# Splitting the last chunk of the output weights one unit later, and the low parts of two q-weight chunks on GpSimd

## The chip, the cores and the metric

The kernel runs on one core of a Trainium2 chip. The core has five engines that run side by side, each through its own list of instructions in order: TensorE (PE in the profile, its weight loads PEld), VectorE (DVE), ScalarE (ACT), GpSimd (POOL) and SyncE (SP), which here only issues DMA transfers. The metric is the device time of one execution in microseconds, lower is better. The time before is the median of three runs; one further execution was taken by the profiler, and all rows below come from it.

## The reference

Two linear attentions, A and B, with the same input `x` (2048 tokens, 448 features, 16 heads of 28) and their own weights; a gate per token mixes them:

```python
def attention(x, wqkv, w_phi, wo):
    q, k, v = heads(x @ wqkv)                      # 16 heads of 28
    pq, pk = q @ w_phi, k @ w_phi                  # per head, 28 x 28
    phi_q = concat(softmax(pq), softmax(-pq))      # 56 features
    phi_k = concat(softmax(pk), softmax(-pk))
    kv, z = phi_k^T @ v, sum_over_tokens(phi_k)
    o = (phi_q @ kv) / (phi_q @ z + 1e-6)
    return merge(o) @ wo
g = sigmoid((A_x * gate_w).sum(-1))
out = g * attention(A_x, A...) + (1 - g) * attention(A_x, B...)
```

Both attentions read `A_x`. (The excerpt is shortened; `heads` and `merge` stand for reshapes and transposes.)

## The kernel before

**Precision by two parts.** Large products keep float32 accuracy by splitting an operand into a high part, which ScalarE makes by a copy to a rounded type (`high_w`, L133; `high_folded`, L202), and a low part, the difference, which VectorE or GpSimd makes (`low_w`, L136; `low_folded`, L208). A projection of two token tiles (`proj`, L225) is 22 matmuls over such parts.

**Folded weights.** The feature map `w_phi` is multiplied into the q and k weights on the chip. For A this is `fold` (L153, L158, L159). For B the strips of the weights are loaded, multiplied on TensorE (`fold_strips`, L181), transposed by VectorE (`turn_strips`, L189), stored to DRAM (`td`, L191) and loaded again in chunks (`load_folded`, L198), and the chunks are split by `high_folded` and `low_folded`. For the q weights of B there are four chunks, and only two buffers, `bd` and `wps`: chunks 2 and 3 are loaded into the same buffers once the low parts of chunks 0 and 1 have been made.

**Units.** The 16 token tiles are handled in 8 units of two tiles. Every engine gets its instructions in the order in which the program below issues them; a manual schedule keeps that order.

- *Stage 1* (first loop, L476) takes the k and v side of A: per unit the k projection, `k_shift` (L239 to L242: maximum and differences on VectorE, the mirrored half on GpSimd), `k_exp` (L246, ScalarE), `k_sums` (L255, L256 on VectorE, L264 twice on GpSimd: phi of k), the v projection and `v_out` (L272, ScalarE), and a unit late `kv_acc` (L289, TensorE: phi_k against v). Between these lies work that prepares later stages: the split of the output weights, the folded k weights of B, and the first q units of A.
- *Stage 2* (second loop, L584) takes k and v of B and, beside it, q of A: `q_front` (L316, L318 on VectorE, stores L325 to DRAM from the sync and ScalarE queues), `q_load` (L333, the exchanged layout back), `q_exp0` (L341, ScalarE), `q_min` (L345 on VectorE, L349 on GpSimd), `q_exp1` (L356), `q_turn` (L359, VectorE, into `wtb[k % 2]`), `num` (L371, TensorE), then for the unit before `a_turn` (L576, VectorE), `n_rec` (L383 VectorE, L388 and L389 GpSimd), `n_den` (L396), `weights` (L403, L404 GpSimd), `n_mul` (L409) and `a_add` (L413, GpSimd). `weights` needs the gates, which unit 0 computes (L566 to L568) and passes through DRAM (L570, L572).
- *Stage 3* is a written-out list of steps (`STEPS`): q of B, and the output products (L839) against the split output weights.

**The split of the output weights.** The weights are held as seven chunks in DRAM (`wos`). `load_wo(c)` (L459) loads a chunk into a half of `wtb[c // 2 % 2]`; `high_wo(c)` makes the high part on ScalarE (L133), `low_wo(c)` the low part on GpSimd (L136) and then issues two stores to DRAM from the sync queue (L468, L469):

```python
WOS = {3: (0, 1), 5: (4, 5, 2, 3), 6: (6,)}    # L473: unit of stage 1 -> chunks
...
for c in WOS.get(u, ()):                       # L524, after k_exp(u)
    high_wo(c)
    low_wo(c)
```

The load of chunk 6 is issued at the end of unit 5 (L536), when the stores of chunks 2 and 3, whose buffer it takes, have landed; behind it on the sync queue stand the strips of the q weights of B (L539), then, in unit 6, the q stores and the q load of A's second q unit (`FRONTS`, L474). ScalarE and GpSimd meet chunk 6 in unit 6 ahead of `q_exp0(0)`, `q_min(0)` and `q_exp1(0)` (L549 to L552), and GpSimd ahead of `k_sums(6)`, which the program issues in unit 7 ahead of `k_shift(7)`.

**The low parts of chunks 2 and 3 of B's q weights.** Their high parts are made in unit 1 of stage 2 (L595), their low parts on VectorE in unit 2 (L634), after the turn of q and before the `a_turn` of unit 3. They are first needed by the projection that unit 6 of stage 2 issues.

Buffers in PSUM are three pairs of banks that rotate (`two_tile`), so a projection also waits until the engines have read the one before the last but one.

Of the kernel before, what the change touches and what calls it, by code (L numbers as in the profile page):

```python
# [49 lines left out]
def hedgehog_mix(ctx: ExitStack, tc: tile.TileContext, xd, wv, wkt, wqt, wphi, wo, cmask, cpmask, out):  # L50


    nc = tc.nc
# [44 lines left out]
    wq = [wp_.tile([P, 2, 4, D], F32R, name="wqa"), None]  # L98
# [42 lines left out]
    def low_wv(b, c, eng):  # L141
        low_w(wvr[c], wvs[b][:, 0, c], wvs[b][:, 1, c], eng)
# [3 lines left out]
    def two_tile(i=None):  # L146
        if i is None:
            i = turn[0] = (turn[0] + 1) % 3
        return twos[i].tile([P, 2, 512], F32, name=f"two{i}")
# [35 lines left out]
    def turn_strips(wt, ts, i):  # L185
        t = wt[:, :4 * D]
        o = t.rearrange("p (j i w m) -> p i w j m", i=2, w=2, m=HP)
        for j, ps in enumerate(ts):
            nc.vector.transpose(o[:, j], ps[:, :, :D].rearrange("p w (j m) -> p w j m", m=HP))  # L189
        for g in range(4):  # L190
            nc.sync.dma_start(td[i][:, g * P:g * P + P].rearrange("(j t) x -> t j x", t=HP),  # L191
                              t[HP * g:HP * g + HP].rearrange("t (j x) -> t j x", x=P))
# [7 lines left out]
    def high_folded(bufs, dst, cs):  # L200
        for c in cs:
            nc.scalar.activation(dst[:, 0, c].rearrange("p (h f) -> p h f", f=DH),  # L202
                                 bufs[c].rearrange("p (h m) -> p h m", m=HP)[:, :, :DH], AF.Copy)

    def low_folded(bufs, dst, cs, eng):
        for c in cs:
            h, l = [dst[:, i, c].rearrange("p (h f) -> p h f", f=DH) for i in range(2)]
            eng.tensor_tensor(l, bufs[c].rearrange("p (h m) -> p h m", m=HP)[:, :, :DH], h.bitcast(F32), OP.subtract)  # L208
# [7 lines left out]
    def proj(u, w, ps, order=None):  # L216
        n = w.shape[3]
        for i, j in order or [(i, j) for i in range(2) for j in range(11)]:
            if i is None:
                warm(j)  # L220
                continue
            t = 2 * u + i
            x, o = xg[t // 4], (t % 4) * P
            xc, k, wc = TERMS[j]
            nc.tensor.matmul(ps[:, i, :n], x[:, xc, o:o + P], w[:, k, wc], start=j == 0, stop=j == 10)  # L225
        return ps
# [17 lines left out]
    def k_exp(k):  # L244
        for s in range(2):
            nc.scalar.activation(es[k][:, s], es[k][:, s], AF.Exp)  # L246
# [19 lines left out]
    def k_sums(k):  # L266
        k_sums0(k)
        k_sums1(k)
# [12 lines left out]
    def kv_acc(k):  # L281
        b, u = divmod(k, NU)
        v, phi = vs[k % 2], phis.pop(k)
        for w in range(2):
            for g in range(4):
                for r in range(4):
                    h = 4 * r + g
                    hs = (w * H + h) * DH
                    nc.tensor.matmul(kvp[b][32 * r:32 * r + DH + 1, g], v[:, w, h // 2, h % 2], phi[:, :, hs:hs + DH],  # L289
                                     start=(u == 0 and w == 0 and g == 0), stop=(u == NU - 1 and w == 1),  # L290
                                     skip_group_check=True)

    def state_copy(b):
        nc.scalar.activation(kvs[b][:, :, :, :DH], kvp[b].rearrange("p g s f -> p s g f"), AF.Copy)
# [9 lines left out]
    def state_turn(b):  # L304
        state_turn0(b)
        state_turn1(b)
# [20 lines left out]
    def q_front(k, ps):  # L327
        q_diff(k, ps)
        q_store(k, nc.sync)
        q_store(k, nc.scalar)  # L330

    def q_load(k):
        nc.sync.dma_start(tq[k % 2].rearrange("p c g w f -> p (c g w f)"), qd[k].rearrange("r t c x -> (r t) (c x)"))  # L333
# [6 lines left out]
    def q_exp0(k):  # L340
        nc.scalar.activation(eq[:, 0, :, :, :DH], tview(k), AF.Exp)  # L341

    def q_least(k):
        mn = work.tile([P, 4, 8], F32, name="qmn")
        nc.vector.tensor_reduce(mn, tq[k % 2].rearrange("p c g w f -> p c (g w) f"), AX.X, OP.min)  # L345
        return mn

    def q_rest(k, mn):
        nc.gpsimd.tensor_tensor(eq[:, 1, :, :, :DH], mn.rearrange("p c a -> p a c")[:, :, :, None].to_broadcast([P, 8, 4, DH]),  # L349
                                tview(k), OP.subtract)  # L350

    def q_min(k):
        q_rest(k, q_least(k))

    def q_exp1(k):
        nc.scalar.activation(eq[:, 1, :, :, :DH], eq[:, 1, :, :, :DH], AF.Exp)  # L356

    def q_turn(k):
        nc.vector.transpose(wtb[k % 2], eq.rearrange("p s a c f -> p (s a c f)"))  # L359
        eTs[k] = wtb[k % 2].rearrange("p (s g t) -> p s g t", s=2, g=4)  # L360
# [30 lines left out]
    def n_rec(k):  # L391
        n_rec0(k)
        n_rec1(k)

    def n_den(k):
        nc.vector.reciprocal(sms[k][2], sms[k][2])  # L396

    def weights(k, eng):
        b, u = divmod(k, NU)
        rs, dd, den = sms[k]  # L400
        gt = gate[:, b, :, 2 * u:2 * u + 2].rearrange("p c n -> p n c")
        d4 = den.rearrange("p r (n c) -> p r n c", n=2)
        eng.tensor_tensor(d4, d4, gt[:, None].to_broadcast([P, 4, 2, 4]), OP.mult)  # L403
        eng.tensor_tensor(dd, rs, den[:, :, None, :].to_broadcast([P, 4, 2, 8]), OP.mult)  # L404

    def n_mul(k, lo=0, hi=8):
        c3 = cview(k).rearrange("p r s a m -> p (r s) a m")[:, :, lo:hi, :DH]
        dd = sms[k][1].rearrange("p r s a -> p (r s) a")[:, :, lo:hi, None]
        nc.gpsimd.tensor_tensor(c3, c3, dd.to_broadcast([P, 8, hi - lo, DH]), OP.mult)  # L409
# [51 lines left out]
    def high_wo(c):  # L461
        st = wo_part(c)
        high_w(st[0], st[1].bitcast(F32R))
# [6 lines left out]


    WVS = {2: (0, 1), 3: (2, 3)}
    WOS = {3: (0, 1), 5: (4, 5, 2, 3), 6: (6,)}  # L473
    FRONTS = {2: 0, 5: 1}  # L474
    pq = None
    for u in range(NU):  # L476
# [45 lines left out]
        for c in WVS.get(u, ()):  # L522
            low_wv(1, c, nc.gpsimd)
        for c in WOS.get(u, ()):  # L524
            high_wo(c)
# [48 lines left out]
    def a_turn(k):  # L574
        for i, t in enumerate(nums[k]):
            nc.vector.transpose(ctr[k % 2][:, 1024 * i:1024 * i + 1024], t.rearrange("p i t -> p (i t)"))  # L576
        nums.pop(k)
# [6 lines left out]
    for u in range(NU):  # L584
        k = NU + u
        f, m, n = u + 2, u + 1, u - 1
        if u == 2:
            ctr[1] = mid.tile([P, 2048], F32, name="ctr")
        pq = proj(f % NU, wq[f // NU], two_tile())
        if n >= 0:  # L590
            a_turn(n)
            n_rec(n)
        q_exp0(m)
        if u == 1:
            high_folded(fq, wq[1], (2, 3))  # L595
        q_min(m)
        if u == 0:
            turn_strips(wtqb, pf, 1)
        q_exp1(m)
        if n >= 0:  # L600
            n_den(n)
            weights(n, nc.gpsimd)
            if u > 1:
                n_mul(n)
        else:
            k_sums(k - 1)
        q_front(f, pq)
        q_load(f)
        pk = proj(u, wk[1], two_tile())
        if u == 0:  # L610
            kv_acc(k - 1)
            state_copy(0)
        else:
            k_sums(k - 1)
            if u == 1:
                n_mul(n)
        k_shift(k, pk)
        if u == 0:
            state_turn(0)
            q_turn(m)  # L620
        pv = proj(u, wvs[1], two_tile())
        v_out(k, pv)
        k_exp(k)
        if u == 0:
            fq = [wp_.tile([P, 512], F32, name=n) for n in ("bd", "wps")] * 2
            for cs in ((0, 1), (2, 3)):
                load_folded(1, fq, cs)
                if cs[0] == 0:
                    high_folded(fq, wq[1], cs)
                    low_folded(fq, wq[1], cs, nc.gpsimd)  # L630
        else:
            q_turn(m)
        if u == 2:
            low_folded(fq, wq[1], (2, 3), nc.vector)  # L634
        if u == NU - 1:
            woh, wol = [wp_.tile([P, 7, D], F32R, name=n) for n in ("wkb", "wvb")]
            for w, d in ((woh, wod[0]), (wol, wod[1])):
                nc.sync.dma_start(w.bitcast(F32), d)
        if n >= 0:
            a_add(n)  # L640
        if u == 4:
            nc.gpsimd.tensor_scalar(gate[:, 1], gate[:, 0], -1.0, 1.0, op0=OP.mult, op1=OP.add)
        ts = nums[u] = [two_tile(), two_tile()]
        num(u, [t[:, i] for t in ts for i in range(2)])
        if u == 0:
            gates()
        else:
            kv_acc(k - 1)
# [261 lines left out]
```

## Time and profile before

| | us |
|---|---|
| median of 3 runs (lowest, highest) | 355.02 (354.36, 358.86) |
| profiled execution | 357.44 |
| its span | 355.7 |
| TensorE busy in the span | 345.7 |
| VectorE busy | 276.2 |
| GpSimd busy | 264.6 |
| ScalarE busy | 122.0 |

The profile names a group of instructions by line, engine, operation, and the program's names of what is written and read. In a timeline a row has the start in us from the span's start, the time from the first start to the last end, engine, line, operation, shape and count; in brackets stands the idle time of the engine before it and what ended that. "SPq" is the sync queue's issue of a DMA; the transfer itself runs on. The chain of waits is followed back from the last instruction, at each step to what released it or to the instruction before it on its engine. Rows of stretches give the busy time of each engine, with the number of instructions in parentheses, the granted clock of TensorE as a share of full speed, the busy share of the DMA engines and the bytes that they moved per second.

### The profile page before, as it was taken

How to read it: one execution, taken by the hardware profiler on the slowest of the kernel's cores; microseconds unless marked ns; L12 is line 12 of the kernel's file. 1: busy time of each engine (PE TensorE's matmuls, PEld its weight loads, DVE VectorE, ACT ScalarE, POOL GpSimd, SP SyncE). 2: the span in 40 equal slices, each digit the busy share in tenths (PEclk: the TensorE clock that was granted, in tenths of full speed). 3: DMA queues.
4: the chain of work that ended last, by engine and by line, in shares of the span. 5: the costliest groups of instructions: out<-in, count | busy, mean ns of one | idle time of the engine just before them, and what ended most of it. 6: DMA issues, size and time to landing. Idle time of an engine off the chain costs nothing.

```text
span 355.7 us, 8516 instructions
## 1 busy us (share of the span) xinstructions
PE 345.7 (97%) x3599; PEld 301.6 (85%) x3599; DVE 276.2 (78%) x319; ACT 122.0 (34%) x176; POOL 264.6 (74%) x230
## 2 busy tenths in 40 slices
PE   8999999999969999999999999999999999999995
PEld 7999888889867888888798989888888978888894
DVE  4328765666776769799999898899899999988840
ACT  4525445126334052222244131412224454334331
POOL 2453799795574346995989788896779999999850
PEclk9999999999996999999999999999999999999999
DMA  8795236865744633141322333158672562664111
GB/s 242 224 332 143 103 99 201 216 163 185 187 101 110 162 102 100 55 131 53 103 77 82 105 105 98 61 188 330 170 233 68 153 177 77 178 173 129 53 53 52
DMA packets 39022, 49.58 MB, mean 139 GB/s; under 512 B 11848, under 2 KB 32168, under 8 KB 38696
## 3 DMA queue, kind: packets, MB, share of 16 engines
q1 hardware_dynamic: 33832, 44.90, 42.7%
q10 hardware_dynamic: 5152, 4.13, 3.7%
q8 instruction: 28, 0.46, 0.5%
q14 instruction: 10, 0.08, 0.1%
HBM read 29.27 MB, written 21.36 MB: 142 GB/s over the span
## 4 chain that ended last, share of the span: by engine, by line
PE 73%; DVE 11%; POOL 8%; DMA 3%; issue 3%; ACT 1%; POOLq 0%; DVEq 0%; ACTq 0%
PE two L225 44%; PE out L839 16%; PE two L371 4%; PE kv L289 3%; POOL e L264 3%; DMA wtb<-wos 2%; PE two L153 2%; PE two L434 2%; POOL wva L409 2%; DVE wva L576 1%; DVE wtb L359 1%; DVE sm L255 1%; DMA wod<-wtb 1%; PE two L181 1%; DVE wka L208 1%
## 5 line engine op out<-in xcount | busy, mean ns | idle before, releaser
L225 PE MATMUL two<-wka,xg 128*128 128x448 f32 x352 | 73.8, 365 | 0.0
L225 PEld LDWEIGHTS two<-wka,xg 128*128 128x128 f32 x352 | 65.1, 188 | 6.4 <-issue 0.8
L264 POOL TENSOR_TENSOR e<-e,rs 128x896 f32<-128x896 f32 x32 | 53.8, 1705 | 16.3 <-DVE rs L256 16.3
L272 ACT ACTIVATE vs<-two 128x896 f32<-128x896 f32 x16 | 14.7, 918 | 82.3 <-PE two L225 77.8
L255 DVE TENSOR_REDUCE sm<-e 128x32 f32<-128x896 f32 x32 | 33.0, 1071 | 8.7 <-ACT e L246 8.7
L225 PE MATMUL two<-wva,xg 128*128 128x450 f32 x176 | 39.3, 373 | 0.1
L225 PE MATMUL two<-wqa,xg 128*128 128x448 f32 x176 | 39.2, 379 | 0.0
L225 PEld LDWEIGHTS two<-wqa,xg 128*128 128x128 f32 x176 | 33.6, 194 | 5.0 <-ACT e L246 1.5
L359 DVE STREAM_TRANSPOSE wtb<-xrb 128x2048 f32<-128x2048 f32 x16 | 36.6, 2289 | 1.5 <-ACT xrb L356 1.5
L246 ACT ACTIVATE e<-e 128x896 f32<-128x896 f32 x32 | 28.7, 945 | 26.5 <-POOL e L242 26.4
L225 PE MATMUL two<-wvb,xg 128*128 128x448 f32 x176 | 37.2, 366 | 0.0
L242 POOL TENSOR_TENSOR e<-mx,e 128x896 f32<-128x896 f32 x16 | 27.3, 1706 | 13.0 <-DVE mx L241 12.8
L225 PE MATMUL two<-wkb,xg 128*128 128x448 f32 x176 | 36.7, 363 | 0.1
L225 PEld LDWEIGHTS two<-wva,xg 128*128 128x128 f32 x176 | 33.1, 190 | 3.2 <-issue 0.3
L225 PEld LDWEIGHTS two<-wvb,xg 128*128 128x128 f32 x176 | 33.0, 188 | 2.8
L225 PEld LDWEIGHTS two<-wkb,xg 128*128 128x128 f32 x176 | 32.9, 188 | 2.8 <-DVE wva L576 0.5
L839 PE MATMUL out<-wkb,e 128*128 128x448 f32 x154 | 34.7, 369 | 0.1
L839 PEld LDWEIGHTS out<-wkb,e 128*128 128x128 f32 x154 | 28.5, 188 | 4.1 <-issue 0.8
L349 POOL TENSOR_TENSOR xrb<-qmn,tq 128x896 f32<-128x896 f32 x16 | 28.2, 1762 | 3.5 <-issue 1.9
L409 POOL TENSOR_TENSOR wva<-wva,cdd 128x896 f32<-128x896 f32 (+1 forms) x12 | 26.5, 2212 | 0.8
L409 POOL TENSOR_TENSOR ctr<-ctr,cdd 128x896 f32<-128x896 f32 (+1 forms) x12 | 26.5, 2212 | 0.6
L239 DVE TENSOR_REDUCE mx<-two 128x32 f32<-128x896 f32 x16 | 16.8, 1048 | 11.8 <-PE two L225 11.8
(117 smaller groups left out, 586.3 us busy)
## 6 DMA issues: line engine op xcount, KB each, us to landing
tq<-qd SPq DMA_DIRECT2D x16, 448.0 KB
qd<-uq ACTq DMA_DIRECT2D x32, 112.0 KB
qd<-uq SPq DMA_DIRECT2D x32, 112.0 KB
od<-wva SPq DMA_DIRECT2D x8, 448.0 KB
wqa<-od SPq DMA_DIRECT2D x8, 448.0 KB
wod<-wtb SPq DMA_DIRECT2D x14, 224.0 KB
xrb<-in_xt SPq DMA_DIRECT2D x2, 1024.0 KB
out<-bd SPq DMA_DIRECT2D x8, 224.0 KB
```

The costliest lines, as they stand in the source:

```text
L225: nc.tensor.matmul(ps[:, i, :n], x[:, xc, o:o + P], w[:, k, wc], start=j == 0, stop=j == 10)
L239: nc.vector.tensor_reduce(mx[:, 0], p4, AX.X, OP.max)
L242: nc.gpsimd.tensor_tensor(e5[:, 1], mx[:, 1, :, :, None].to_broadcast([P, 2, H, DH]), e5[:, 0], OP.subtract)
L246: nc.scalar.activation(es[k][:, s], es[k][:, s], AF.Exp)
L255: nc.vector.tensor_reduce(sm[:, s], e[:, s].rearrange("p (h f) -> p h f", f=DH), AX.X, OP.add)
L264: nc.gpsimd.tensor_tensor(e3, e3, rs[:, s, :, None].to_broadcast([P, HA, DH]), OP.mult)
L272: nc.scalar.activation(v[:, :, :, :, :DH].rearrange("p w j q f -> p w (j q) f"), hb(ps[:, :, :D]), AF.Copy)
L349: nc.gpsimd.tensor_tensor(eq[:, 1, :, :, :DH], mn.rearrange("p c a -> p a c")[:, :, :, None].to_broadcast([P, 8, 4, DH]), tview(k), OP.sub ...
L359: nc.vector.transpose(wtb[k % 2], eq.rearrange("p s a c f -> p (s a c f)"))
L371: nc.tensor.matmul(banks[r][32 * g:32 * g + 32, 256 * s:256 * s + 256], kvt[b][32 * r:32 * r + 32, s, g], eT[32 * r:32 * r + 32, s, g], st ...
L409: nc.gpsimd.tensor_tensor(c3, c3, dd.to_broadcast([P, 8, hi - lo, DH]), OP.mult)
L839: nc.tensor.matmul(outs[t % 2][:, :D], (hi, lo)[x][:, c], w[:, c], start=x == 0 and n == 0 and c == 0, stop=x == 1 and c == 6)
```

## The change

Chunk 6 of the output weights is split in unit 7 of stage 1 instead of unit 6: its high part on ScalarE, its low part on GpSimd and its two stores on the sync queue move, the load does not. The low parts of chunks 2 and 3 of the folded q weights of B are made on GpSimd in unit 1 of stage 2, behind that unit's `q_min`, instead of on VectorE in unit 2. Nothing is added or taken away.

```diff
-    WOS = {3: (0, 1), 5: (4, 5, 2, 3), 6: (6,)}
+    WOS = {3: (0, 1), 5: (4, 5, 2, 3), 7: (6,)}
...
         if u == 1:
             high_folded(fq, wq[1], (2, 3))
         q_min(m)
+        if u == 1:
+            low_folded(fq, wq[1], (2, 3), nc.gpsimd)
...
         else:
             q_turn(m)
-        if u == 2:
-            low_folded(fq, wq[1], (2, 3), nc.vector)
         if u == NU - 1:
```

## The prediction

> **What bounds the kernel now.** I read the page's table of engines first, then the chain of waits, then the order of time on each engine around the two edits. Stage 1 is the first loop over units, stage 2 the second, stage 3 the written-out list.
>
> ```profile
> PE 345.7 (97%) x3599; PEld 301.6 (85%) x3599; DVE 276.2 (78%) x319; ACT 122.0 (34%) x176; POOL 264.6 (74%) x230
> ```
>
> TensorE is busy nearly throughout, so an edit on other engines pays only where TensorE waits or runs slowly. The chain of waits (start us, us, what) leaves TensorE at two places that the change touches:
>
> ```profile
> 91.55 8.00 DMA wtb<-wos
> ...
> 100.31 1.16 POOL wtb L136
> ...
> 103.13 3.37 POOL e L264 x2
> ...
> 160.87 3.09 DVE wka L208 x2
> 163.96 2.30 DVE wva L576 x2
> ```
>
> The first place is unit 6 of stage 1: the load of chunk 6 of the output weights takes 8.00 us, GpSimd's split of it (L136) waits for that, and the normalising of the k features of that unit (L264) waits behind on the same engine. The second is unit 2 of stage 2, where the low parts (L208) take 3.09 us of VectorE. TensorE in order of time, from three stretches:
>
> ```profile
> 58.44 1.51 PE L181 MATMUL two<-wtb,wps 28*32 28x448 f32 x32
> ...
> 80.10 4.76 PE L225 MATMUL two<-wqa,xg 128*128 128x448 f32 x22
> 84.70 4.57 PE L225 MATMUL two<-wka,xg 128*128 128x448 f32 x22
> ...
> 99.15 4.66 PE L225 MATMUL two<-wva,xg 128*128 128x450 f32 x22
> 106.55 1.72 PE L289 MATMUL kv<-e,vs 128*29 128x56 f32 x64 [2.74 <-POOL e L264]
> 108.20 1.81 PE L181 MATMUL two<-ctr,wps 28*32 28x448 f32 x32
> 109.94 6.02 PE L225 MATMUL two<-wqa,xg 128*128 128x448 f32 x22
> 115.79 4.57 PE L225 MATMUL two<-wkb,xg 128*128 128x448 f32 x22
> 120.29 0.99 PE L289 MATMUL kv<-e,vs 128*29 128x56 f32 x64
> ...
> 127.42 4.75 PE L225 MATMUL two<-wqa,xg 128*128 128x448 f32 x22
> ...
> 160.33 4.75 PE L225 MATMUL two<-wqa,xg 128*128 128x448 f32 x22
> ...
> 177.90 4.75 PE L225 MATMUL two<-wqa,xg 128*128 128x448 f32 x22
> ...
> 193.82 4.75 PE L225 MATMUL two<-wqa,xg 128*128 128x448 f32 x22
> ```
>
> At 103.81 TensorE stops for 2.74 us, and what follows is slow: the k-v products take 1.72 instead of 0.99, the strips 1.81 instead of 1.51, the projection 6.02 instead of 4.76, together 2.29 more. Waiting and slowness make 5.03 us. The stretches of 1 us (PE, PEld, DVE, ACT, POOL busy, granted clock, DMA share, GB/s) name the slowness:
>
> ```profile
> 105.00:106.00 1.00, 0.00 (x0) 0.00 (x0) 1.00 (x1) 0.03 (x1) 1.00 (x1) 0.96 1.00 215
> 106.00:107.00 1.00, 0.45 (x20) 0.45 (x24) 0.51 (x1) 0.00 (x0) 1.00 (x2) 0.50 0.83 253
> 107.00:108.00 1.00, 1.00 (x56) 1.00 (x48) 0.19 (x1) 0.00 (x0) 1.00 (x1) 0.50 1.01 385
> ...
> 112.00:113.00 1.00, 1.00 (x5) 0.90 (x4) 1.00 (x2) 0.00 (x0) 0.00 (x0) 0.62 0.00 0
> ```
>
> The granted clock falls to half shortly before 106, some 2.1 us after TensorE stopped, and is back only after 112. In stage 2 a unit whose start is not held back takes 15.92 us (177.90 to 193.82). Units 1 and 2 together take 32.91 (127.42 to 160.33), 1.07 over two such units; unit 3 takes 17.57, 1.65 over.
>
> **Part 1, the split of chunk 6 a unit later.** What frees: GpSimd and ScalarE no longer meet the load in unit 6. The rows that then decide, from the timelines of VectorE, GpSimd, ScalarE and the sync queue:
>
> ```profile
> 94.96 1.79 ACT L246 ACTIVATE e<-e 128x896 f32<-128x896 f32 x2
> ...
> 98.06 0.55 DVE L256 RECIPROCAL rs<-sm 128x64 f32<-128x64 f32 x1
> ...
> 101.61 1.09 DVE L241 TENSOR_REDUCE mx<-e 128x32 f32<-128x896 f32 x1
> ...
> 104.05 0.34 SPq L333 DMA_DIRECT2D tq<-qd  x1
> 104.07 0.90 ACT L272 ACTIVATE vs<-two 128x896 f32<-128x896 f32 x1
> ...
> 107.81 1.09 DVE L345 TENSOR_REDUCE qmn<-tq 128x32 f32<-128x896 f32 x1 [1.29 <-DMA tq<-qd]
> ...
> 110.18 2.11 DVE L189 STREAM_TRANSPOSE ctr<-two 128x896 f32<-128x896 f32 x2 [1.29 <-PE two L181]
> ...
> 112.22 2.04 DVE L255 TENSOR_REDUCE sm<-e 128x32 f32<-128x896 f32 x2
> ...
> 114.99 3.37 POOL L264 TENSOR_TENSOR e<-e,rs 128x896 f32<-128x896 f32 x2 [4.21 <-DVE rs L256]
> ```
>
> L264 of unit 6 needs the reciprocals that end at 98.61, so it can run to about 102.0, before TensorE arrives at 103.81: the 2.74 wait goes, and with it the 2.29 of half clock. TensorE then goes on: 0.92 of k-v products, 1.45 of strips, 4.60 (80.10 to 84.70) and 4.50 (115.79 to 120.29) of projections bring it to the next k-v products (unit 7) at 115.3 instead of 120.29.
>
> What is late next: those products need L264 of unit 7, and the way to it goes over VectorE, which keeps its order: L345, which needs the loaded q values (issued at 104.05, an issue that the edit does not move), then L189, L255, L256. From the rows: L345 ends at 108.90; L189 to the start of L255 is 2.04, from there to L264 2.77, and 3.37 for L264: 117.08, a new wait of 1.8 us. That is one end. The other: the two stores of chunk 6 now come after that load instead of beside it; the three stretches from 105 to 108 moved 853 KB, of which 448 KB are this load, so by the 385 GB/s of the last of them half of the 3 us can go, say 0.9 us (an estimate); the wait is then 0.9. I take the middle, 1.4, the rows giving no nearer one. The gain of part 1 is 5.03 - 1.4 = 3.6 us, between 3.2 and 4.1.
>
> The moved instructions in unit 7: the exponentials before them on ScalarE can start when L272 is done (104.97) and take 1.79; high part 0.6 to 107.4; low part 1.16 on GpSimd (the row of L136) to 108.5. Behind it GpSimd has the q step that waits for L345's end (108.0 to 108.9), ScalarE the load of q (about 107), so at most half a microsecond of either shows, off the chain through VectorE. The two stores stay behind the q load on the sync queue, which next waits for L189's end near 111; they have landed long before the turn of stage 2's unit 0 overwrites that buffer, some 10 us on. I cost all this at nothing.
>
> **Part 2, the low parts from VectorE in unit 2 to GpSimd in unit 1.** The rows of GpSimd, ScalarE and the sync queue:
>
> ```profile
> 129.16 1.15 POOL L208 TENSOR_TENSOR wka<-bd,wka 128x448 fp32r<-128x448 f32 x1 [3.21 <-ACT wka L202]
> ...
> 131.45 1.13 SPq L198 DMA_DIRECT2D wps<-td  x2
> ...
> 134.47 1.76 POOL L349 TENSOR_TENSOR xrb<-qmn,tq 128x896 f32<-128x896 f32 x1 [0.26 <-DVE qmn L345]
> ...
> 136.00 0.58 ACT L202 ACTIVATE wka<-wps 128x448 fp32r<-128x448 f32 x1 [2.45 <-DMA wps<-td]
> ...
> 138.56 0.27 POOL L403 TENSOR_TENSOR cden<-cden,gate 128x32 f32<-128x32 f32 x1 [2.33 <-DMA gate<-gd]
> ...
> 139.43 3.37 POOL L264 TENSOR_TENSOR e<-e,rs 128x896 f32<-128x896 f32 x2 [0.20 <-DVE rs L256]
> ...
> 166.92 0.36 POOL L388 TENSOR_TENSOR cdd<-wva,crs 128x64 f32<-128x64 f32 x1 [3.44 <-DVE crs L383]
> ...
> 173.56 3.37 POOL L264 TENSOR_TENSOR e<-e,rs 128x896 f32<-128x896 f32 x2
> ```
>
> Added: 2 x 1.15 = 2.3 us on GpSimd behind L349, which ends at 136.23. The second needs the high part that ends at 136.58; both end near 138.55, and until 138.56 GpSimd was waiting for the gates. They fit to a few hundredths; 0.2 more stand before L264. Cost: nothing to 0.3; without the cover of that gate wait they would still end at 138.55, and only a later second high part shows.
>
> Removed: VectorE's turn at 163.96 (L576) moves up 3.09. GpSimd's L388, idle 3.44 before, starts up to 3.1 earlier, and L264 at 173.56 with it: it ends near 173.9. TensorE, without its 1.65 of excess, reaches the k-v products at about 175.5, so the products' own work is the limit. Gain 1.5, between 0.9 (if GpSimd starts late as in part 1) and 1.65. The excess of units 1 and 2 lies ahead of the removed instructions and stays.
>
> Sum: 3.6 + 1.5 = 5.1 us; ends 3.2 + 0.9 - 0.3 = 3.8 and 4.1 + 1.65 = 5.75. After 177.90 the units run at TensorE's pace, so the gain reaches the end. The profiled execution took 357.44 us (span 355.7 and 1.74 around it): 352.3 by its own time. The median of the runs shown, 355.02, lies 2.42 lower; I take the same 5.1 off: **349.9 us**.
>
> **Whether the new wait costs the clock.** In the rows, 2.1 us without a matmul were followed by half clock. A wait of 0.9 to 1.8 is below that, but not by much. [...] By the rows alone, if some 1.8 us is already enough, the half clock comes on top, as below.
>
> **Rivals.**
> *Half the gain* (0.20): the half clock comes back at the new wait, or the runs without profile did not have it: their median lies 2.42 below the profiled time, as much as half clock costs (2.29). Either takes 2.29 off: 352.2. For it: that coincidence, and a wait near 2 us; against: one run at 358.86 lies above the profiled one.
> *More* (0.08): no new wait, and units 1 and 2 lose their 1.07 too: 5.03 + 1.65 + 1.07 = 7.75, 347.3. Against: nothing removed lies ahead of them.
> *GpSimd blocked, slower* (0.06): in its new place the second low part stands in line for the last load of q weights (issued by 132.6, used at 136.00). Each microsecond by which this lands later than about 136 delays L264 and TensorE alike; before, only ScalarE waited. If it takes 8.0 us as the load at 91.55 did, it lands at 140, L264 starts 3.2 late, TensorE waits 3.1, beyond the 2.1 after which the clock fell: 5.4, as much as the gain. From 8 us on the kernel is slower; at 9 us 356.3.
> *It does not do what it says* (0.06): the load of chunk 6 lands so late that unit 7 waits as unit 6 did, or another row keeps L264 of unit 6 back: only part 2 is left, 353.5. Against: the load had landed by 99.6, 8 us before its new use.
>
> **Chances.** The forecast has 0.60, its own range 349.3 to 351.2. The range 348.0 to 353.7 takes in the half gain and the change that half fails. Two per cent, about what a measurement can tell from no change, is 7.1 us: faster than 347.9 only in the case of more gain, 0.08; slower than 362.1 only if the blocked GpSimd costs twice what is reckoned, 0.02; within, 0.90.
>
> **What would show it.** Right: in unit 7 of stage 1 no wait of the k-v products (L289) and clock 1.00 throughout; a wait of 0.9 to 1.8 us in stage 2's unit 0, released by L264; L208 only on GpSimd, before the gates; no L208 ahead of L576 on VectorE and a unit 3 of about 16 us. Wrong: half clock anywhere in the middle; L403 or L264 of unit 1 later against TensorE than before; the k-v products of unit 6 waiting still.

## The result, and the profile after

The changed kernel takes 352.0 us (median of 20 runs, 350.62 to 357.02), the kernel before 355.81 (20 runs, 354.19 to 358.86); the ratio is 0.9905 with a 95% interval of 0.9878 to 0.9933. It is faster by 3.4 to 3.8 us, less than two per cent. The forecast was 349.9, its range 348.0 to 353.7. The profiled execution of the changed kernel took 354.63 us with a span of 352.8, against 357.44 and 355.7.

TensorE of the changed kernel in order of time (start us, us, engine, line, what, count, in brackets the idle time before it and what ended it), where the prediction showed that of the kernel before:

```profile
103.72 0.99 PE L289 MATMUL kv<-e,vs 128*29 128x56 f32 x64
104.67 1.16 PE L181 MATMUL two<-ctr,wps 28*32 28x448 f32 x32
105.76 4.74 PE L225 MATMUL two<-wqa,xg 128*128 128x448 f32 x22
110.34 4.67 PE L225 MATMUL two<-wkb,xg 128*128 128x448 f32 x22
117.37 1.65 PE L289 MATMUL kv<-e,vs 128*29 128x56 f32 x64 [2.37 <-POOL e L264]
118.95 5.63 PE L225 MATMUL two<-wvb,xg 128*128 128x448 f32 x22
...
125.94 4.76 PE L225 MATMUL two<-wqa,xg 128*128 128x448 f32 x22
...
159.16 4.76 PE L225 MATMUL two<-wqa,xg 128*128 128x448 f32 x22
...
175.08 4.75 PE L225 MATMUL two<-wqa,xg 128*128 128x448 f32 x22
```

Set start against start with the rows before. The k-v products of unit 6 (L289) no longer wait, and the k projection of stage 2's unit 0 starts at 110.34 instead of 115.79: 5.45 us gained. Then the k-v products of unit 7 wait 2.37 us, they and the v projection (L225 into `wvb`) run slowly, and the q projection of unit 1 starts at 125.94 instead of 127.42: of the 5.45 only 1.48 are left. Units 1 and 2 take 33.22 us together (32.91 before), unit 3 takes 15.92 (17.57 before): 2.82 ahead at 175.08, against a span shorter by 2.9. After that nothing differs: from this mark to the end are 177.7 us here and 177.8 before.

What TensorE no longer waits for (L264 of unit 6, at 98.71), and what it now waits for (L264 of unit 7, at 113.97), from the timelines of the other engines of the changed kernel:

```profile
95.43 0.92 SPq L325 DMA_DIRECT2D qd<-uq  x2
98.71 3.36 POOL L264 TENSOR_TENSOR e<-e,rs 128x896 f32<-128x896 f32 x2 [2.11 <-DVE rs L256]
...
104.49 0.34 SPq L333 DMA_DIRECT2D tq<-qd  x1
107.03 0.34 SPq L468 DMA_DIRECT2D wod<-wtb  x1
107.09 1.16 POOL L136 TENSOR_TENSOR wtb<-wtb 128x448 fp32r<-128x448 f32 x1 [2.60 <-ACT wtb L133]
...
108.17 1.09 DVE L345 TENSOR_REDUCE qmn<-tq 128x32 f32<-128x896 f32 x1 [3.31 <-DMA tq<-qd]
109.17 2.10 DVE L189 STREAM_TRANSPOSE ctr<-two 128x896 f32<-128x896 f32 x2
...
113.97 3.35 POOL L264 TENSOR_TENSOR e<-e,rs 128x896 f32<-128x896 f32 x2 [2.88 <-DVE rs L256]
```

The new wait comes the way that the prediction named: the q load, L345, L189, the sums, L264. But the load, issued at 104.49, is there only at 108.17, 3.68 us later, although the stores of chunk 6 are issued only at 107.03; with those stores beside it it had taken 3.76 in the kernel before (104.05 to 107.81). And the clock fell. Stretches of 1 us of the changed kernel (columns as before: busy time of five engines, granted clock, DMA share, GB/s):

```profile
116.00:117.00 1.00, 0.00 (x0) 0.00 (x0) 0.96 (x2) 0.00 (x0) 1.00 (x1) 1.00 0.94 183
117.00:118.00 1.00, 0.63 (x32) 0.63 (x36) 1.00 (x1) 0.00 (x0) 0.32 (x1) 0.75 1.01 274
...
120.00:121.00 1.00, 1.00 (x5) 0.90 (x4) 1.00 (x1) 0.00 (x0) 1.00 (x2) 0.54 0.52 79
```

TensorE stopped at 115.0, was at work again at 117.37, and only then, at 117.5, half clock set in; it lasted to 120.9.

**In how many executions the clock falls.** Each run has a mean granted clock. No run lies between 0.995 and 0.997, so two groups can be told apart (executions that the comparison leaves out as disturbed are not counted). The kernel before is counted over the 32 runs that stood beside the experiments.

| kernel | clock up to 0.995: runs, mean us | clock 0.997 and more: runs, mean us |
|---|---|---|
| before | 22, 356.4 | 10, 354.3 |
| changed | 4, 354.7 | 15, 351.9 |

So the gain has two pieces: 2.4 us between executions in which the clock holds, and the rest because it falls in 4 of 19 instead of 22 of 32. Below, a run in which the clock held is one with a mean of 0.997 or more. The mean clock does not say where it fell; the profiled executions of the two kernels show it at the waits above, and that of the kernel before once more behind the last matmul (0.58 from 355.0 on), where TensorE has no work left. In p1_only and p2_only below, profiled at means of 0.999 and 0.997, the stretches of 1 us around the waits (114 to 119 and 103 to 107) all have a clock of 1.00. Not every long run is explained by the clock: one of the 15 of the changed kernel took 355.77 at a mean of 1.0.

### The profile page after: what moved, and what is told of

Read it like the earlier page. It is cut to its first block, busy times and chain, and to the rows that moved or that the text cites. A ratio compares the mean times of both kernels' runs of the same rounds, so it can differ in the third digit from the quotient of the medians.

```text
span 352.8 us, 8518 instructions
## 1 busy us (share of the span) xinstructions
PE 343.4 (97%) x3599; PEld 300.4 (85%) x3599; DVE 274.1 (78%) x317; ACT 122.1 (35%) x176; POOL 266.5 (76%) x232
## 4 chain that ended last, share of the span: by engine, by line
PE 69%; POOL 10%; DVE 9%; DMA 6%; issue 2%; ACT 2%; SPq 1%; POOLq 0%; ACTq 0%; DVEq 0%
PE two L225 42%; PE out L839 16%; POOL e L264 4%; PE two L371 4%; PE kv L289 3%; DMA qd<-uq 2%; PE two L153 2%; DVE sm L255 2%; DMA xrb<-in_xt 1%; DMA tq<-qd 1%; POOL xg L115 1%; POOL wva L409 1%; PE kv L371 1%; POOL ctr L409 1%; DVE wva L770 1%
## 5 line engine op out<-in xcount | busy, mean ns | idle before, releaser
L225 PE MATMUL two<-wka,xg 128*128 128x448 f32 x352 | 73.8, 366 | 0.0
L225 PEld LDWEIGHTS two<-wka,xg 128*128 128x128 f32 x352 | 65.2, 188 | 6.4 <-issue 0.8
L264 POOL TENSOR_TENSOR e<-e,rs 128x896 f32<-128x896 f32 x32 | 53.8, 1703 | 17.0 <-DVE rs L256 17.0
L225 PE MATMUL two<-wva,xg 128*128 128x450 f32 x176 | 38.9, 371 | 0.7 <-ACT wva L133 0.6
L225 PE MATMUL two<-wvb,xg 128*128 128x448 f32 x176 | 38.1, 372 | 0.0
L225 PE MATMUL two<-wqa,xg 128*128 128x448 f32 x176 | 37.9, 370 | 0.0
L225 PE MATMUL two<-wkb,xg 128*128 128x448 f32 x176 | 36.7, 363 | 0.0
L225 PEld LDWEIGHTS two<-wva,xg 128*128 128x128 f32 x176 | 33.0, 189 | 4.1 <-ACT wva L133 1.0
L225 PEld LDWEIGHTS two<-wvb,xg 128*128 128x128 f32 x176 | 33.7, 192 | 3.0
L225 PEld LDWEIGHTS two<-wqa,xg 128*128 128x128 f32 x176 | 32.5, 188 | 4.1 <-ACT e L246 0.7
L225 PEld LDWEIGHTS two<-wkb,xg 128*128 128x128 f32 x176 | 32.9, 188 | 2.5 <-DVE ctr L189 0.2
L371 PE MATMUL two<-wtb,kvt 32*32 32x256 f32 x768 | 24.7, 385 | 0.1
```

Source lines behind the costliest of these rows:

```text
L264: nc.gpsimd.tensor_tensor(e3, e3, rs[:, s, :, None].to_broadcast([P, HA, DH]), OP.mult)
L371: nc.tensor.matmul(banks[r][32 * g:32 * g + 32, 256 * s:256 * s + 256], kvt[b][32 * r:32 * r + 32, s, g], eT[32 * r:32 * r + 32, s, g], st ...
```

## The experiments

**The parts alone.** Two theories stood against each other: two gains that add, or one of them alone.

```diff
 p1_only: the kernel before, and
-    WOS = {3: (0, 1), 5: (4, 5, 2, 3), 6: (6,)}
+    WOS = {3: (0, 1), 5: (4, 5, 2, 3), 7: (6,)}
```

> Only the split of chunk 6 a unit later; the low parts stay on VectorE in unit 2. My theory (two independent gains): the wait of the k-v products of unit 6 and its half clock are gone, the wait in stage 2's unit 0 is there as in the changed kernel (2.4 us and half clock after it), unit 3 of stage 2 keeps its 1.65 us of excess: 1.5 us more than the changed kernel, about 353.5, 2.3 less than before. Rival (the whole gain comes from VectorE's relief): as before, 355.8. Rival (the parts hang together, the earlier VectorE is what pays): over 354.5.

Measured: 352.89, ratio 0.9924 (0.9889 to 0.9959). Its profiled execution, TensorE and the way to the wait:

```profile
94.31 0.86 SPq L325 DMA_DIRECT2D qd<-uq  x2
103.03 0.34 SPq L333 DMA_DIRECT2D tq<-qd  x1
...
106.37 1.08 DVE L345 TENSOR_REDUCE qmn<-tq 128x32 f32<-128x896 f32 x1 [1.68 <-DMA tq<-qd]
...
115.58 0.99 PE L289 MATMUL kv<-e,vs 128*29 128x56 f32 x64 [0.82 <-POOL e L264]
...
122.61 4.74 PE L225 MATMUL two<-wqa,xg 128*128 128x448 f32 x22
...
155.60 4.76 PE L225 MATMUL two<-wqa,xg 128*128 128x448 f32 x22
...
173.20 4.75 PE L225 MATMUL two<-wqa,xg 128*128 128x448 f32 x22
```

The wait is there, as expected, but 0.82 long and without half clock: here the q stores were issued 1.1 us earlier than in the changed kernel's execution, and what stands behind them came 1.1 to 1.8 earlier. Up to this place the two kernels have the same instructions, so the length of the new wait changes from execution to execution, with the time at which the q load lands. Unit 3 keeps its excess (173.20 - 155.60 = 17.60).

```diff
 p2_only: the kernel before, and
+        if u == 1:
+            low_folded(fq, wq[1], (2, 3), nc.gpsimd)      # behind q_min(m)
...
-        if u == 2:
-            low_folded(fq, wq[1], (2, 3), nc.vector)
```

> Only the low parts to GpSimd in unit 1; chunk 6 is split in unit 6 as before. My theory: the wait at 103.8 and its half clock stay, unit 3 of stage 2 takes 15.9 us instead of 17.6: 1.5 us less than before, about 354.3. Rival (GpSimd pays what VectorE saves): as before, 355.8, with the excess of units 1 and 2 grown by over 1 us. Rival (all of the gain is here): 352.

Measured: 353.06, ratio 0.9903 (0.9872 to 0.9934): 2.7 less than before, where 1.5 was expected; 354.3 would be a ratio of 0.996, outside the interval. TensorE of the profiled execution:

```profile
105.04 0.99 PE L289 MATMUL kv<-e,vs 128*29 128x56 f32 x64 [1.64 <-POOL e L264]
...
123.31 4.76 PE L225 MATMUL two<-wqa,xg 128*128 128x448 f32 x22
...
156.44 4.76 PE L225 MATMUL two<-wqa,xg 128*128 128x448 f32 x22
...
172.35 4.75 PE L225 MATMUL two<-wqa,xg 128*128 128x448 f32 x22
```

Unit 3 takes 15.91, 1.66 less than in the kernel before; units 1 and 2 take 33.13, 0.22 more: 1.4 together, the size expected of part 2. The wait of unit 6 is still there, at 1.64 instead of 2.74, and the clock held: that is where the rest comes from in this execution, and the edit does not touch it. Between executions in which the clock held the difference is 1.7 (352.6, four runs, against 354.3); the clock fell in two of the six. Whether part 2 makes the fall rarer, or these six met fewer by chance, stays open.

By the plain medians the parts do not add: 2.8 and 2.7 alone, 3.8 together. These medians mix executions with and without the fall. With the clock held, part 1 alone gives 1.3 (353.0, nine runs), part 2 alone 1.7, both 2.4. They add but for 0.6, which is no more than the scatter of so few runs; units 1 and 2 do not explain it, for their loss with both parts (0.31) is that of the parts alone (0.08 and 0.22).

**The new wait.** The theory: L264 of unit 7 is late because VectorE stands at L345, for data that L264 does not need.

```diff
 sums_first: the changed kernel, and in stage 2
+        if u == 0:
+            turn_strips(wtqb, pf, 1)
+            k_sums(k - 1)
         q_min(m)
...
-        if u == 0:
-            turn_strips(wtqb, pf, 1)
         q_exp1(m)
...
-        else:
-            k_sums(k - 1)
```

> The changed kernel, and in unit 0 of stage 2 the turn of the strips and the sums of the k features (L189, L255, L256, L264) stand ahead of the step that waits for the loaded q values (L345, L349). My theory (the new wait is VectorE's order: L345 waits for the load, and L264 behind it): L264 ends near 114.1, before TensorE comes at 115.0, no wait there and no half clock: 2.4 us less than the changed kernel where the clock had held, 3.9 less where it had not; 348.1 to 349.6. Rival (the sums wait for something else, the exponentials or the strips): as the changed kernel, 352. Rival (the q step, now later, holds up GpSimd or the turn at 119.8): the wait moves to num or to unit 1, less than 1 us gained.

Measured: 350.72, ratio 0.9837 (0.9806 to 0.9867), and the clock held in all six runs. VectorE, GpSimd and TensorE of its profiled execution:

```profile
108.08 2.04 DVE L255 TENSOR_REDUCE sm<-e 128x32 f32<-128x896 f32 x2
110.62 1.03 DVE L345 TENSOR_REDUCE qmn<-tq 128x32 f32<-128x896 f32 x1
...
110.84 3.37 POOL L264 TENSOR_TENSOR e<-e,rs 128x896 f32<-128x896 f32 x2 [2.54 <-DVE rs L256]
...
114.91 0.99 PE L289 MATMUL kv<-e,vs 128*29 128x56 f32 x64
```

No wait, and L264 ends at 114.21, as reckoned. The wait was VectorE's order, and it cost the changed kernel 1.3 us by the medians (352.0 to 350.7), 2.4 by the ratios (0.9905 to 0.9837). The time is 1.1 us above the expected span, which took the 2.37 us of one profiled execution for the usual length of the wait. Between executions in which the clock held the difference is 1.2 (351.9 to 350.6); that would be the usual length, an estimate that no trace shows by itself.

```diff
 before_sums: the kernel before, and in stage 2
+        if u == 0:
+            turn_strips(wtqb, pf, 1)
+            k_sums(k - 1)
         q_min(m)
-        if u == 0:
-            turn_strips(wtqb, pf, 1)
...
-        else:
-            k_sums(k - 1)
```

> The kernel before, with the sums ahead of the q step in unit 0 of stage 2 and neither part of the change. My theory: without the later split TensorE still waits for L264 of unit 6 (1.6 to 2.8 us) and comes to the next k-v products so late that L264 of unit 7 was there already: as before, within 0.5 us of it. Rival (the order of VectorE alone is the gain): 2 us less or more than that.

Measured: 355.71, ratio 0.9998 (0.997 to 1.0026). TensorE of its profiled execution:

```profile
106.93 0.99 PE L289 MATMUL kv<-e,vs 128*29 128x56 f32 x64 [3.28 <-POOL e L264]
...
119.63 0.99 PE L289 MATMUL kv<-e,vs 128*29 128x56 f32 x64
```

As expected: as long as unit 6 waits, unit 7 does not, and the order on VectorE is worth nothing. Part 1 did open the new wait.

```diff
 fill_wait: the changed kernel, and in stage 2, unit 0
-        pk = proj(u, wk[1], two_tile())
+        pk = proj(u, wk[1], two_tile(), [(i, j) for i in (0, 1, 0)[:3 if u == 0 else 2] for j in range(11)])
```

> The changed kernel, and TensorE does the first of the two token tiles of the k projection of stage 2's unit 0 a second time (11 matmuls, 2.3 us, the same values into the same place), so that it works through the time in which it waited 2.37 us. My theory (half clock is the price of the idle time, not of the stage): clock 1.00 through that place, the k-v products 0.99 and not 1.65, the v projection 4.63 and not 5.63: 1.6 us less than the changed kernel in an execution with half clock, nothing in one without: 350.4 to 352. Rival (the half clock comes at that place whatever TensorE does, or the added work shows): as the changed kernel or up to 2.3 us more, 352 to 354.3.

Measured: 352.37, ratio 0.9893 (0.9862 to 0.9924), clock 0.998 and more in all six runs. TensorE of its profiled execution:

```profile
110.11 6.78 PE L225 MATMUL two<-wkb,xg 128*128 128x448 f32 x33
116.81 0.99 PE L289 MATMUL kv<-e,vs 128*29 128x56 f32 x64
117.73 4.76 PE L225 MATMUL two<-wvb,xg 128*128 128x448 f32 x22
```

Where TensorE worked through the wait the clock held, the k-v products took 0.99 and the projection 4.76. Six runs alone prove little, since the clock held in 15 of 19 of the changed kernel; but in the five variants here in which TensorE does not wait at this place and chunk 6 is split late (sums_first, this one, and stores_first, sums_gates and all_three below) it held in 28 of 28. So half clock is taken as the price of the idle time. On the median the edit gains nothing, 0.4 over the expected span and inside the rival's 352 to 354.3: the added work shows, for 2.2 us of it replace a wait that by the estimate above is usually shorter.

**Where the load's lateness comes from.** The q stores stand on the sync queue behind the load of chunk 6 and the strips.

```diff
 stores_first: the changed kernel; load_wo(6) and load_strips move
+            if u == 6:
+                load_wo(6)
+                load_strips(wtqb, wqt[1])
             q_load(FRONTS[u - 1])                         # behind q_front
...
-            load_wo(6)                                    # in unit 5
...
-            wtqb = load_strips(mid.tile([P, 2048], F32, name="ctr"), wqt[1])
+            wtqb = mid.tile([P, 2048], F32, name="ctr")
```

> The changed kernel with the order of VectorE as it is, but on the sync queue the stores of A's second q unit are issued ahead of the load of chunk 6 and of the strips (they stood behind both, and so behind the landing of the stores of chunks 2 and 3). My theory (the new wait is the late landing of the q load at about 106.4 to 108.2, which follows the issue of these stores one for one): the q load is issued at 95 to 97, L345 starts right behind L359 near 104.9, L264 ends near 114.2, no wait at the k-v products of unit 7: 350.7, as with the sums ahead of the q step. Rival (the load then stands behind the strips on the DMA engines and lands no earlier): as the changed kernel, 352. Rival (chunk 6 or the strips land later and hold TensorE at 103.7): over 352.

Measured: 350.34, ratio 0.986 (0.9833 to 0.9888), the time expected, but not in the way expected. Sync queue, VectorE and TensorE:

```profile
93.31 1.82 SPq L173 DMA_DIRECT2D ctr<-in_wqt  x4
95.24 0.40 SPq L333 DMA_DIRECT2D tq<-qd  x1
...
106.50 1.09 DVE L345 TENSOR_REDUCE qmn<-tq 128x32 f32<-128x896 f32 x1 [1.87 <-DMA tq<-qd]
...
104.44 2.11 PE L181 MATMUL two<-ctr,wps 28*32 28x448 f32 x32
106.48 4.75 PE L225 MATMUL two<-wqa,xg 128*128 128x448 f32 x22
...
115.72 0.99 PE L289 MATMUL kv<-e,vs 128*29 128x56 f32 x64
```

The q load is issued nine microseconds earlier, behind the strips (L173), and is there at 106.50, 11.26 us later, within the 106.37 to 108.17 of the executions with the old order, where it took 3.19 to 4.02 us: as the rival said, it lands no earlier. That the strips' transfer held it is not shown by these rows. TensorE passes the strips' products more slowly (2.04 from start to start instead of 1.09 in the changed kernel) and comes to the k-v products just as L264 ends. In this execution, with a mean clock of 0.998, one long wait became a delay of 1 us, and the load was not early. The rival was right about the load and wrong about the time. Nor does the landing follow the issue of the q stores one for one, as the theory had it: issued at 94.25, 94.28 and 94.31 (the kernel before, fill_wait, p1_only), they were followed by landings at 107.81, 106.99 and 106.37. What sets it from execution to execution stays open.

**What was left in units 1 and 2.** With the new wait gone, VectorE stands idle for the gates. From sums_first:

```profile
124.39 0.57 DVE L567 TENSOR_SCALAR glog<-glog 128x16 f32<-128x16 f32 x1 [3.48 <-ACT glog L566]
```

```diff
 sums_gates: sums_first, and gates() split; in unit 0 of stage 2
         k_shift(k, pk)
         if u == 0:
+            gates0()                     # L566 to L568: the sigmoid
             state_turn(0)
...
-            gates()
+            gates1()                     # the way through DRAM, behind num as before
```

> The changed kernel with the sums ahead of the q step, and the gates (L566 to L568: one step on ScalarE, two on VectorE) computed before the state is copied, not after num; their way through DRAM stays where it is. VectorE waited 3.4 us (before) and 6.2 us (changed) for them with the turn of num (L576) behind. My theory: L576 of unit 1 starts when num of unit 0 ends, some 2 us earlier against TensorE, and units 1 and 2, 0.9 over their 31.84 together, lose most of that: 0.5 to 0.9 us less than with the sums ahead alone, 350.0. Rival (units 1 and 2 are held by GpSimd or by the gates' way through DRAM): no change, 350.7.

Measured: 349.36, ratio 0.9828 (0.9802 to 0.9855). TensorE and VectorE of its profiled execution:

```profile
122.69 4.75 PE L225 MATMUL two<-wqa,xg 128*128 128x448 f32 x22
...
154.54 4.75 PE L225 MATMUL two<-wqa,xg 128*128 128x448 f32 x22
...
122.76 2.38 DVE L578 STREAM_TRANSPOSE wva<-two 128x1024 f32<-128x1024 f32 x2 [0.90 <-PE two L371]
```

The turn of num (L578 in this kernel, L576 above) now waits for TensorE, not for the gates, and units 1 and 2 take 31.85 us, two units without excess; with the sums alone they took 32.90. The 1.05 gained are a little more than the 0.5 to 0.9 expected, and the medians differ by 1.4. This is the best version: 349.36 against 352.0 for the change and 355.73 for the kernel before.

```diff
 all_three: sums_gates, and the lines of stores_first
+            if u == 6:
+                load_wo(6)
+                load_strips(wtqb, wqt[1])
             q_load(FRONTS[u - 1])
...
-            load_wo(6)                                    # in unit 5
...
-            wtqb = load_strips(mid.tile([P, 2048], F32, name="ctr"), wqt[1])
+            wtqb = mid.tile([P, 2048], F32, name="ctr")
```

> The sums ahead of the q step, the early gates and the q stores ahead of chunk 6 and the strips, all on the changed kernel. My theory: the stores add nothing once the sums do not wait for the load: as with sums and gates, 350.0. Rival (the load's late landing also holds GpSimd's q step and the turn at 119): 0.5 to 1 us less.

Measured: 349.47, ratio 0.9836 (0.9809 to 0.9863): nothing more than sums_gates, as expected.

## Why the prediction was right, and where not

**Right.** The place and the mechanism of the first gain: without chunk 6 ahead of it on GpSimd, L264 of unit 6 runs from 98.71 and TensorE does not stop at 103.7. That the moved instructions of chunk 6 cost nothing: its low part (L136) ran at 107.09, in a gap of GpSimd, its stores stayed behind the q load. That the next thing late would be the k-v products of unit 7, over the q load, L345, L189 and the sums. The second gain: unit 3 lost its whole excess, 1.65. The fit of the low parts on GpSimd, whose rows in the changed kernel are

```profile
134.80 1.16 POOL L208 TENSOR_TENSOR wka<-bd,wka 128x448 fp32r<-128x448 f32 x1
135.91 1.16 POOL L208 TENSOR_TENSOR wka<-wps,wka 128x448 fp32r<-128x448 f32 x1
137.65 0.27 POOL L403 TENSOR_TENSOR cden<-cden,gate 128x32 f32<-128x32 f32 x1 [0.57 <-DMA gate<-gd]
```

with 0.57 us to spare before the gates' data. Against TensorE these data, and L264 behind them, come some 0.6 and 0.3 us later than before, one of the signs of being wrong that the prediction named; GpSimd was waiting for the data, so the low parts are not the cause in this execution, and units 1 and 2 lose the 0.3 that the prediction allowed. The rival of the blocked GpSimd did not come: the last q weights landed in time, at 134.70, where the DMA released L202 on ScalarE.

**The step that failed most** is the one from the profiled execution to the median, "I take the same 5.1 off". It gives every execution of the kernel before the whole 2.29 us of half clock to lose. The runs show that the clock fell in 22 of 32, at a cost of 2.1 between the means of the two groups, 1.4 on average, and that in the changed kernel it still falls in 4 of 19, at 2.8, 0.6 on average: some 0.9 of the 2.29 was to be had. The profiled execution of the kernel before, with a mean clock of 0.990, is of the kind that loses the most: only five of the 22 lie as low, at 0.989, the others at 0.992 to 0.994. The rest of the miss is the start: the median of the kernel before was 355.02 over three runs and is 355.81 over twenty.

**The size of the new wait**, "0.9 to 1.8, I take the middle", was right on average by the estimate of 1.2, but it is no single size: 0.82 in p1_only and 2.37 in the changed kernel. The row that the upper end started from, the load's arrival at 107.81, was taken for fixed; it was 106.37, 106.57, 106.99, 107.81 and 108.17 in the five profiled executions with the old order on VectorE and on the sync queue. The lower end came from the bytes that the stores of chunk 6 moved beside the load: with them the load took 3.76 and 4.02 us (p2_only), without them 3.68, 3.34 (p1_only) and 3.19 (fill_wait), so about half of that 0.9 is there, by these five. In the changed kernel's profiled execution TensorE also came 0.3 us earlier than reckoned, for the strips took 1.09 us from start to start, not 1.45. With the wait of 2.37 the half clock came back and cost 1.6 us, the prediction's own sign of being wrong. The 2.1 us after which it reckoned with half clock were the delay of one fall; in two other executions the fall came 2.5 and 4.3 to 5.3 us after the stop (last section).

**The rival that came** is the half gain. Both its mechanisms did their part: in some executions the clock falls at the new wait, and in 10 of 32 the kernel before had no fall to lose. Its price fits the profiled pair, which differs by 2.8 us (357.44 to 354.63). That its 352.2 also lies so near the measured 352.0 is partly luck: it is a gain of 2.8 off 355.02, and measured is a gain of 3.4 to 3.8 off 355.81. That the time lies inside the range is owed to the range having been made wide enough for this rival.

## What to carry to other kernels

When an edit frees an engine that works in order, look at what stands next on that engine, and whether the one who is waiting needs it: here a reduction that waited for a DMA stood ahead of sums that were already possible, and reordering them was worth 1.3 to 2.4 us on top of the change's 3.4 to 3.8. A wait on the bottleneck engine cost more than its length where the clock fell with it: here 1.6 us on top of 2.37, and 2.29 on top of 2.74, while the profiled executions with waits of 0.82 and 1.64 us kept the clock. So where a trace shows such a fall, turning one long wait into short ones is worth a try; no run here did only that. And a single profiled execution may be one draw out of two: before its waits are taken off a median, the mean clock of the other runs tells how often they happen.

## What the runs showed of the hardware

Waits of TensorE of 0.82 us (p1_only) and 1.64 us (p2_only) left the clock at 1.00, in the stretches from 114 to 119 and from 103 to 107; with waits of 2.37 (the changed kernel), 2.74 (the kernel before) and 3.28 us (before_sums) it fell to 0.50. The fall did not follow the stop by a fixed time: it came 2.1 us after it in the kernel before, with TensorE still waiting, and 2.5 us after it in the changed kernel, with TensorE at work again. In before_sums, whose wait ran from 103.65 to 106.93, it came between 108 and 109, 4.3 to 5.3 us after the stop:

```profile
107.00:108.00 1.00, 1.00 (x66) 0.91 (x69) 0.00 (x0) 0.00 (x0) 1.00 (x1) 1.00 0.99 376
...
109.00:110.00 1.00, 1.00 (x17) 0.50 (x2) 0.41 (x1) 1.00 (x2) 0.00 (x0) 0.50 0.00 0
...
111.00:112.00 1.00, 1.00 (x4) 0.88 (x4) 1.00 (x2) 0.21 (x1) 0.00 (x0) 0.58 0.00 0
```

Half clock lasted 3.4 us in the changed kernel (117.5 to 120.9), 6.84 in the kernel before (105.92 to 112.76) and 2.8 to 3.8 in before_sums (to 111.8), although TensorE worked through most of it. These ends are estimates from the clocks of the 1 us stretches, taking each as a mix of 1.00 and 0.50.

What decides whether a wait lets the clock fall, and when, these executions do not show: no run varied the length of the wait on purpose, and between 1.64 us, where the clock stayed, and 2.37, where it fell, no wait was traced. Nor do they show why one kernel does both, for the executions without a trace have only their mean clock.
